# A fourth buffer for r, k, v and the turned r, and flag sums placed among the last products

## The chip, the core and the metric

The kernel runs on one core of a Trainium2 chip. The metric is the device time of one execution in microseconds. TensorE is called PE here, VectorE DVE, ScalarE ACT, GpSimd POOL and SyncE SP. Each runs its own instructions in the order in which they were written and waits for the others through semaphores. SP issues nearly all of the DMAs, in one queue; POOL issues the scatters.

## What is computed

Three layers in a row: a linear attention with a decaying state (one state matrix for each batch and head), a softmax-weighted layer with a norm, and a mixture of eight experts of which each token takes one.

```python
for t in range(S):                       # B, H, S, D = 4, 8, 768, 48
    cur = np.einsum('bhd,bhe->bhde', u[None] * kt, vt)
    y[:, :, t] = np.einsum('bhd,bhde->bhe', rt, state + cur)
    state = w[None, :, :, None] * state + np.einsum('bhd,bhe->bhde', kt, vt)
...
h = x @ w_in                             # x: 3072 x 384, h: 3072 x 1024
solu = h * softmax(h)
x = ((solu - mean) / sqrt(var + 1e-6) * g_ln) @ w_out
...
e = argmax(x @ w_gate)                   # 8 experts
out = gate * (relu(x @ w1[e]) @ w2[e])
```

## The kernel before

The 3072 tokens are cut into 24 tiles of 128. For each tile i the rows of r, k and v come in one DMA (`load_rkv`, line 173, 576 KB) into one of three tiles `rkv0` to `rkv2`, and r, turned so that the head's elements lie on the partitions, comes in another (`load_r`, line 177, 256 KB) into one of three tiles `rT0` to `rT2`. Tile i takes buffer i mod 3. The last of the `rT` tiles serves once, at the start, as scratch for the table of decay powers (`tables`, line 368, turned by PE at line 374).

What happens to a tile: k is scaled by powers of the decay (`kp`, line 414, mostly on POOL) and turned on PE (line 454, copied by ACT at line 461 into `kT`); rT is scaled (line 457, mostly POOL); PE makes the scores (line 470), DVE masks them (lines 476 and 478), PE makes the output (`attend`, lines 500 to 507) and the update of the state (line 518), DVE advances the state (lines 526, 528) and writes the output (`av`, lines 428, 512). ACT squares the rows of r, k, v for a check of their size (line 411; DVE takes some of them at line 408). Then y is split into two half-precision parts (`yy`, lines 541 and 545) and turned by a DMA transpose on SP (line 549); `mm1` (line 576, 18 products of 512 columns) and, after the softmax and the norm, a second DMA transpose on SP (line 652) and `mm2` (line 678, 24 products of 392 columns) follow. The row of each token is scattered to its expert (line 729). In the first 90 us w_in and w_out are loaded by SP (line 187), checked, converted and folded by ACT, DVE and PE. The split of w_in into two half-precision parts is line 235 on DVE.

The nine groups of experts come after: 256 rows and the rest of the expert that stands first, then seven further experts, each with first products (line 977), the rectified halves `hh` (ACT, line 988) and `hl` (DVE, line 991, called rlo in the plan), second products (lines 1002 and 1020), a scaling on ACT (line 1008) and a scatter by POOL (line 1052).

At the end a flag says if any check failed. `marks2` (lines 812 to 816, DVE) brings the checks of each partition together, `flags2` (line 820, PE) sums them over the partitions, `judge2` (lines 824 to 831, DVE) makes the flag `fli`. Every engine loads the flag (line 1426) and branches on it (line 1428) past a slower way of computing everything, to the end of the program (line 1595).

What sets the order: before anything is issued, a planner (`plan`) takes all operations with their costs, dependencies and a due time (`first`). Among the operations that could start within a short time of the earliest it takes the one with the smallest due time, and the resulting order is that of the instructions on each engine. Its dependencies for a load are written with the tables' numbers (`X["rkv"]` and `X["rT"]`, both 3): the load of tile i may come after the last readers of tile i-3. The real wait of a load is set later, by the tile that it writes. On SP the loads stand in one queue with the loads of weights and both kinds of transposes.

## Time and profile before

| What | Value |
|---|---|
| Median of 3 runs | 563.65 us (559.81 to 568.21) |
| The profiled execution | 562.63 us |
| Its span, first to last instruction | 560.9 us |
| PE busy, share of the span | 529.7 us, 94% |
| DVE busy | 424.2 us, 76% |
| ACT busy | 396.0 us, 71% |
| POOL busy | 263.2 us, 47% |
| Mean granted clock of TensorE | 0.982 |

The span is what the profile covers; the execution's own time is 1.7 us longer. The busy time of PE is that of products whose ends are modelled. A wait is put down to what ended last before the waiting instruction began. "kp" and "rT" are names of tiles, "mm" is either of the first two layers' products, "emm" an expert's.

### The profile page before, as it was taken

The page shows a single profiled execution, that of the slowest core. Times are in us where ns is not written, and L with a number is a line of the kernel's source. Part 1 is how long each engine was busy: PE and PEld are TensorE (multiplying, and loading weights), DVE is VectorE, ACT ScalarE, POOL GpSimd, SP SyncE. Part 2 cuts the span into 40 slices and gives each one's busy share as a digit, 9 for nine tenths or more (in the row PEclk, how much of TensorE's full clock was granted, in tenths as well). Part 3 has the DMA queues.
Part 4 walks back from the last instruction along what each step waited for, and adds up shares of the span by engine and source line. Part 5 has one row for each costly group of instructions (what it writes and reads, how often), then busy time and mean ns, then how long its engine had stood idle before and what let it go on. Part 6 is the DMA issues. An engine that isn't in the chain of part 4 may idle for free.

```text
span 560.9 us, 10536 instructions
## 1 busy us (share of the span) xinstructions
PE 529.7 (94%) x3867; PEld 350.1 (62%) x3867; DVE 424.2 (76%) x718; ACT 396.0 (71%) x780; POOL 263.2 (47%) x265
## 2 busy tenths in 40 slices
PE   4899999999999999989999999999999999999990
PEld 2787675655767666666665567864555555666770
DVE  7789899998888979999976866566696787744120
ACT  4968987988677685766765874998696978596220
POOL 5346765977988867768952230130013303050310
PEclk9899989999999999999999999999999999999996
DMA  8576793577765685648459726875698986791100
GB/s 284 200 194 205 249 224 98 117 158 143 203 143 142 130 181 128 159 116 151 98 91 185 201 87 205 262 196 179 164 238 195 251 220 168 198 281 48 36 16 25
DMA packets 116396, 92.17 MB, mean 164 GB/s; under 512 B 92284, under 2 KB 102486, under 8 KB 115952
## 3 DMA queue, kind: packets, MB, share of 16 engines
q1 hardware_dynamic: 111376, 81.93, 57.9%
q0 software_dynamic: 4960, 9.49, 5.5%
q8 instruction: 32, 0.52, 0.4%
q14 instruction: 28, 0.23, 0.1%
HBM read 57.19 MB, written 12.55 MB: 124 GB/s over the span
## 4 chain that ended last, share of the span: by engine, by line
PE 68%; DVE 13%; ACT 6%; DMA 5%; issue 5%; POOL 1%; SPq 0%; ACTq 0%; DVEq 0%; POOLq 0%
PE emm L977 16%; PE mm L678 12%; PE mm L576 11%; PE emm L1020 8%; PE emm L1002 7%; PE scores L470 3%; PE attend L504 2%; PE attend L507 2%; PE update L518 2%; DMA rkv<-in_rkv 2%; DVE yy L545 1%; DMA stage<-in_moe_w 1%; DMA xg<-xs 1%; DMA raw<-in_moe_w_out 1%; DVE vl L449 1%
## 5 line engine op out<-in xcount | busy, mean ns | idle before, releaser
L1052 POOL DMA_INDIRECT out<-o,gt x29 | 37.7, 1299 | 171.6 <-ACT o L1048 97.4
L678 PE MATMUL mm<-wo,zT 128*128 128x392 f16 x576 | 99.3, 329 | 0.5 <-ACT kT L461 0.5
L977 PE MATMUL emm<-exT,w1h 128*128 128x256 f16 (+8 forms) x432 | 98.6, 317 | 0.3 <-DVE hl L991 0.3
L576 PE MATMUL mm<-wi,xT 128*128 128x512 f16 x432 | 97.6, 380 | 0.6 <-DVE AT L478 0.6
L678 PEld LDWEIGHTS <-zT 128*128 128x128 f16 x576 | 54.9, 98 | 38.6 <-issue 1.5
L576 PEld LDWEIGHTS <-xT 128*128 128x128 f16 x432 | 41.8, 99 | 48.1 <-issue 2.0
L977 PE MATMUL emm<-exT,w1l 128*128 128x256 f16 (+8 forms) x216 | 68.5, 317 | 0.0
L977 PEld LDWEIGHTS <-w1h 128*128 128x128 f16 x432 | 41.7, 97 | 25.3 <-issue 0.5
L991 DVE SCALAR_TENSOR_TENSOR hl<-emm,hh 128x928 f16<-128x928 f32 (+8 forms) x32 | 32.2, 1006 | 30.6 <-ACT hh L988 30.6
L988 ACT ACTIVATE hh<-emm 128x928 f16<-128x928 f32 (+8 forms) x32 | 27.1, 847 | 22.0 <-PE emm L977 21.7
L486 POOL TENSOR_TENSOR al<-AT,ah 128x1024 f16<-128x1024 f32 x16 | 37.0, 2311 | 7.1 <-ACT ah L482 6.9
L869 DVE SCALAR_TENSOR_TENSOR w2l<-stage,w2h 128x768 f16<-128x768 f32 x32 | 30.1, 952 | 11.5 <-ACT w2h L865 11.5
L457 POOL TENSOR_TENSOR rT<-rT,trT 128x512 f32<-128x512 f32 x21 | 28.6, 1362 | 21.0 <-DMA rT<-in_rT 16.5
L729 POOL DMA_INDIRECT xs<-row,pos x24 | 28.4, 1185 | 20.7 <-ACT pos L725 12.7
L869 DVE SCALAR_TENSOR_TENSOR w1l<-stage,w1h 128x1024 f16<-128x1024 f32 x24 | 29.3, 1222 | 10.2 <-ACT w1h L865 10.0
L504 PE MATMUL attend<-sdec,rT 128*128 128x96 f32 x160 | 34.1, 298 | 0.0
L1002 PE MATMUL emm<-w2h,hl 128*128 128x384 f16 (+3 forms) x104 | 33.9, 326 | 0.0
L414 POOL TENSOR_TENSOR kp<-rkv,tkm 128x384 f32<-128x384 f32 x23 | 25.1, 1093 | 18.7 <-DMA rkv<-in_rkv 14.8
L1002 PE MATMUL emm<-w2l,hh 128*128 128x384 f16 (+3 forms) x104 | 33.9, 326 | 0.0
L1002 PE MATMUL emm<-w2h,hh 128*128 128x384 f16 (+3 forms) x104 | 33.9, 326 | 0.0
L648 DVE SCALAR_TENSOR_TENSOR z<-e,z 128x1024 f16<-128x1024 f32 x22 | 33.2, 1509 | 0.3 <-ACT z L609 0.3
L470 PE MATMUL scores<-rT,kT 64*128 64x128 f32 x384 | 29.4, 296 | 4.2 <-ACT kT L461 3.4
(260 smaller groups left out, 1357.0 us busy)
## 6 DMA issues: line engine op xcount, KB each, us to landing
rkv<-in_rkv SPq DMA_DIRECT2D x24, 576.0 KB, 4.4
stage<-in_moe_w SPq DMA_DIRECT2D x16, 768.0 KB, 5.6
stage<-in_moe_w SPq DMA_DIRECT2D x8, 1024.0 KB, 5.2
rT<-in_rT SPq DMA_DIRECT2D x24, 256.0 KB, 4.0
stage<-in_moe_w SPq DMA_DIRECT2D x8, 512.0 KB, 4.7
raw<-in_moe_w_in SPq DMA_DIRECT2D x3, 1024.0 KB, 9.0
raw<-in_moe_w_out SPq DMA_DIRECT2D x4, 768.0 KB, 6.0
xs<-zf SPq DMA_DIRECT2D x8, 337.8 KB, 5.6
```

Source lines behind the costliest of these rows:

```text
L470: T.matmul(ps[:, a, j * P:(j + 1) * P], kT[h, j, :], rT[h, j, :], start=True, stop=True)
L486: on[0].tensor_tensor(al, tk.pop(("at", i)), tk["ah", i], op=ALU.subtract)
L504: T.matmul(ps[:, j * 96:j * 96 + 96], rT[:, j, :], sdec[:, j].rearrange("p a d -> p (a d)"), start=True, stop=False, skip_group_check=True)
L576: T.matmul(ps[:, n, :], x[a][:, j, :], wi[b][:, j, n * 512:(n + 1) * 512], start=(j == 0 and m == 0), stop=(j == KD - 1 and m == 2))
L648: V.scalar_tensor_tensor(z[:, 1, :], tk.pop(("e", i)), tk["st", i][:, 10:11] if i is None else ZC, z[:, 0, :], op0=ALU.mult, op1=ALU.subtract)
L678: T.matmul(ps[:, 0:OW], zz[:, a, c, :], wo[b][:, c, :], start=(c == 0 and m == 0), stop=(c == KF - 1 and m == 2))
L869: V.scalar_tensor_tensor(lo, d[:, x], (S1, S2)[m - 1], hi, op0=ALU.mult, op1=ALU.subtract)
L977: T.matmul(ps[:, x, :].rearrange("p (j t) -> p j t", t=d["n"]), a[:, j, fc * P:(fc + 1) * P], d["xT"][:, 0:d["nt"], b, j, 0:d["n"]], start ...
L991: V.scalar_tensor_tensor(cols(d, "hl", q), d.pop(("pm", q)), 0.0, cols(d, "hh", q), op0=ALU.max, op1=ALU.subtract)
L1002: T.matmul(ps[0:n, 0:DM], a[:, c, j * n:j * n + n], b[:, c, :], start=(c == 0 and m == 0), stop=(c == KF - 1 and m == 2))
L1020: T.matmul(ps[:, 0:d["nr"]], a[:, c, m * P:(m + 1) * P], b[:, c, :], start=(c == 0 and x == 0), stop=(c == KF - 1 and x == 2))
L1052: G.indirect_dma_start(out=apart["out"].pop(0), out_offset=bass.IndirectOffsetOnAxis(ap=d["gt"][0:n, j, 1:2].bitcast(U32), axis=0), in_=d. ...
```

## The change

It gives the rows of r, k, v and the turned r one more buffer each, while the planner's dependencies keep the number three. The tables' scratch is the last of the `rT` tiles, so now the fourth. The marks get a dependency on the last rlo of the last expert and a smaller planned cost; the flag sums and the judgement get a due time of -1e9, which puts them ahead of all that could start at the same time.

```diff
-    whole = [one.tile([P, 3, H, D], F32, name=f"rkv{i}") for i in range(X["rkv"])]
-    turned_r = [one.tile([P, 4, P], F32, name=f"rT{i}") for i in range(X["rT"])]
+    whole = [one.tile([P, 3, H, D], F32, name=f"rkv{i}") for i in range(X["rkv"] + 1)]
+    turned_r = [one.tile([P, 4, P], F32, name=f"rT{i}") for i in range(X["rT"] + 1)]
...
-        t = rkv[i] = whole[i % X["rkv"]]
+        t = rkv[i] = whole[i % len(whole)]
...
-        tk["rT", i] = turned_r[i % X["rT"]]
+        tk["rT", i] = turned_r[i % len(turned_r)]
...
-    op("marks2", "dve", 3.5, [... ["marks", "judge"] ...], marks2, first=0)
-    op("flags2", "pe", .3, ["marks2"], flags2, bank="s", until=["judge2"], first=0)
-    op("judge2", "dve", 1.0, ["flags2"], judge2, first=0)
+    op("marks2", "dve", 1.7, [... ["marks", "judge", ("rlo", E, 3)] ...], marks2, first=0)
+    op("flags2", "pe", .3, ["marks2"], flags2, bank="s", until=["judge2"], first=-1e9)
+    op("judge2", "dve", 1.2, ["flags2"], judge2, first=-1e9)
```

On SP the order of the instructions is the same in both kernels; what differs is the buffer that a load writes and what it waits for. SP's queue near the program's start, before (`DMAHW` semaphores tell of landed DMAs, the others of the engine's instructions):

```order
L173 DMA rkv2_144<-in_rkv 128x1152
L187 DMA raw_256<-in_moe_w_in 128x2048 [waits DMAHW0_49]
L177 DMA rT2_147<-in_rT 128x512 [waits DMAHW1_49,DVE_49,PE_49]
L187 DMA raw_329<-in_moe_w_in 128x2048 [waits DMAHW2_49,DMAHW3_49,DVE_49,Activation_49]
L173 DMA rkv0_142<-in_rkv 128x1152 [waits DVE_49,Pool_49]
L177 DMA rT0_145<-in_rT 128x512 [waits DMAHW4_49]
L177 DMA rT1_146<-in_rT 128x512 [waits DMAHW5_49,DMAHW6_49,PE_49,Pool_49]
L187 DMA raw_433<-in_moe_w_out 128x2x768 [waits DMAHW0_49,DVE_49,Activation_49]
L173 DMA rkv1_143<-in_rkv 128x1152 [waits DMAHW7_49,DVE_49]
```

The same rows of the changed kernel:

```order
L173 DMA rkv2_144<-in_rkv 128x1152
L187 DMA raw_258<-in_moe_w_in 128x2048 [waits DMAHW0_49]
L177 DMA rT2_148<-in_rT 128x512 [waits DMAHW1_49]
L187 DMA raw_331<-in_moe_w_in 128x2048 [waits DMAHW2_49,DMAHW3_49,DVE_49,Activation_49]
L173 DMA rkv3_145<-in_rkv 128x1152
L177 DMA rT3_149<-in_rT 128x512 [waits DMAHW4_49,PE_49]
L177 DMA rT0_146<-in_rT 128x512 [waits DMAHW5_49,PE_49,Pool_49]
L187 DMA raw_435<-in_moe_w_out 128x2x768 [waits DMAHW0_49,DMAHW6_49,DVE_49,Activation_49]
L173 DMA rkv0_142<-in_rkv 128x1152 [waits DMAHW7_49,PE_49,Pool_49]
```

The third rT no longer waits for the tables' scratch on DVE and PE, the fourth load of rows waits for nothing, and from there on each load writes the buffer of the tile four back.

On PE one row moves. Before, at the end of the last expert's second products (`hl` and `hh` are the halves of the hidden layer, `fli` the flag):

```order
L1002 LDWEIGHTS hl
L1002 MATMUL emm_6368<-w2h,hl 114x384
L820 MATMUL flags_6398<-g_100,mask 128x47
L1426 TENSOR_LOAD fli
L1428 COMPARE_AND_BRANCH
```

In the changed kernel, after the first 24 of these 72 products:

```order
L1002 LDWEIGHTS hl
L1002 MATMUL emm_6293<-w2h,hl 114x384
L820 MATMUL flags_6340<-g_100,mask 128x47
L1002 LDWEIGHTS hh
L1002 MATMUL emm_6344<-w2h,hh 114x384
```

The sums now stand ahead of 48 products; the load of the flag follows PE's last product. On DVE, ACT and POOL the order is the same as before.

## Rows read from the trace of the kernel before

**Rows 1.** The page: the span

```profile
span 560.9 us, 10536 instructions
```

**Rows 2.** Busy us by stretch: length, PE, PEld, DVE, ACT, POOL; PEclk, DMA, GB/s

```profile
20.00:340.00 320.00, 313.46 (x2531) 213.27 (x2531) 283.41 (x481) 236.37 (x529) 211.14 (x203) 0.98 0.64 153
...
79.00:87.00 8.00, 8.00 (x38) 5.46 (x39) 7.97 (x12) 5.98 (x10) 6.94 (x5) 0.57 0.70 174
40.00:60.00 20.00, 19.66 (x162) 15.74 (x161) 19.66 (x27) 16.33 (x37) 13.63 (x11) 1.00 0.66 206
```

**Rows 3.** PE's waits, 15 to 340 us: who for whom, us, times, longest

```profile
PE scores L470 <- ACT kT L461: 3.4, 3, 1.6
...
PE ktrans L454 <- POOL kp L414: 0.3, 1, 0.3
...
PE rank L712 <- DVE oh L698: 0.2, 1, 0.2
```

**Rows 4.** Waits in SP's queue, the whole span; same columns

```profile
SPq L173 <- DVE av L428: 11.7, 3, 7.8
...
SPq L177 <- PE rank L713: 0.4, 1, 0.4
```

**Rows 5.** POOL's timeline: start, us, instruction, idle time before it and its releaser

```profile
26.49 1.01 POOL L414 TENSOR_TENSOR kp<-rkv,tkm 128x384 f32<-128x384 f32 x1 [7.83 <-DMA rkv<-in_rkv]
...
43.93 1.00 POOL L414 TENSOR_TENSOR kp<-rkv,tkm 128x384 f32<-128x384 f32 x1 [1.93 <-DMA rkv<-in_rkv]
```

**Rows 6.** The chain that ended last, near 176 us: start, us, what

```profile
175.23 1.22 SPq L549
...
176.54 4.71 DMA rkv<-in_rkv
```

**Rows 7.** Timelines of SP's queue and of PE near 40 us

```profile
37.01 1.03 SPq L177 DMA_DIRECT2D rT<-in_rT  x1
39.08 0.33 SPq L173 DMA_DIRECT2D rkv<-in_rkv  x1
...
44.98 0.66 PE L454 MATMUL ktrans<-ident,kp 128*128 128x128 f32 x4 [0.34 <-POOL kp L414]
```

**Rows 8.** Timelines of DVE, PE, POOL and the chain, at the program's end

```profile
535.85 11.71 PE emm L1002 x72
...
539.03 0.14 DVE L816 TENSOR_REDUCE g<-low 128x1 f32<-128x2 f32 x1
...
547.38 0.32 PE L820 MATMUL flags<-g,mask 128*128 128x47 f32 x2
...
548.80 0.15 DVE L831 CAST fli<-fl 128x1 int32<-128x1 f32 x1
...
548.51 1.13 POOL L1052 DMA_INDIRECT out<-o,gt  x1 [2.76 <-ACT o L1008]
```

**Rows 9.** Lines 1426, 1428, 1595 and the scatters: count, ns min/median/max, starts

```profile
L1426 POOLq TENSOR_LOAD <-fli x1: 508/508/508, 549.0 to 549.0; - x1
...
L1428 POOLq EVENT_SEMAPHORE  x6: 17/30/43, 553.9 to 554.3; - x6
...
L1428 POOLq INC_SWDGE_SEM  x1: 1244/1244/1244, 554.4 to 554.4; - x1
...
L1595 POOLq DRAIN  x3: 44/107/4402, 555.7 to 560.7; - x3
...
DMA to landing us min/median/max: 3.7/3.7/5.4
```

**Rows 10.** Timelines of POOL and DVE: the split of w_in

```profile
17.38 1.28 POOL L457 TENSOR_TENSOR rT<-rT,trT 128x512 f32<-128x512 f32 x1 [0.94 <-DMA rT<-in_rT]
...
18.11 1.63 DVE L235 SCALAR_TENSOR_TENSOR wi<-tmp,wi 128x1024 f16<-128x1024 f32 x1
...
42.34 1.21 DVE L235 SCALAR_TENSOR_TENSOR wi<-tmp,wi 128x1024 f16<-128x1024 f32 x1
```

**Rows 11.** The chain: the folding of w_out

```profile
77.41 2.77 PE wout_fold L275 x24
```

More of the change, by code (lines that the diff above doesn't have):

```diff
@@ L1284, in body @@
                 esends.append(("esend", y, j))
-    op("marks2", "dve", 3.5, [k for k in ops if stem(k) == "look"] + [("square", i) for i in range(NT)] + [("hvar", i) for i in range(NT)] + ["marks", "judge"] + [("rhi", y, q) for y in range(E + 1) for q in range(4)] + [("wsq", e, n) for e in range(E) for n in range(4)] + [("xsq", y) for y in range(E + 1)] + [(q, x) for x in range(2) for q in ("woq", "wiq")], marks2, first=0)
-    op("flags2", "pe", .3, ["marks2"], flags2, bank="s", until=["judge2"], first=0)
-    op("judge2", "dve", 1.0, ["flags2"], judge2, first=0)
+    op("marks2", "dve", 1.7, [k for k in ops if stem(k) == "look"] + [("square", i) for i in range(NT)] + [("hvar", i) for i in range(NT)] + ["marks", "judge", ("rlo", E, 3)] + [("rhi", y, q) for y in range(E + 1) for q in range(4)] + [("wsq", e, n) for e in range(E) for n in range(4)] + [("xsq", y) for y in range(E + 1)] + [(q, x) for x in range(2) for q in ("woq", "wiq")], marks2, first=0)
+    op("flags2", "pe", .3, ["marks2"], flags2, bank="s", until=["judge2"], first=-1e9)
+    op("judge2", "dve", 1.2, ["flags2"], judge2, first=-1e9)
     PORT = {"rev", "elo", "wlo", "ylo", "vlo", "zlo", "bits", "wil", "wol", "alo", "decay", "kpow", "ruk", "aval"}
```

## The prediction

> **What bounds the kernel now.** I read the page first, then the busy time of each engine by stretches, the waits of PE and of SP's queue, the chain that ended last, and timelines where a load is late. The span is 560.9 us [rows 1]; the profiled execution took 562.6 us, so 1.7 us lie around the span, and the median of the three runs, 563.65, is 1.0 above that execution. Between 20 and 340 us, where the tiles of r, k, v are used, PE is busy for 313.46 of 320 us [rows 2]. That is the figure to hold on to: nothing that loads data earlier can give PE back more than 320 - 313.46 = 6.5 us in this stretch. The list of what PE waited for there [rows 3] names no DMA at all: eleven entries, 8.6 us together, from 3.4 (the scores, for k turned on ACT) to 0.2 (the one-hot row from DVE). The one that stands behind a load is kp from POOL, 0.3 us.
>
> The loads do wait, and long. SP's queue stands 11.7 us before loads of rkv (line 173) for a reader on DVE [rows 4]; the thirteen entries of lines 173 and 177, down to 0.4, come to 53.4 us, in an order that SP keeps. So the question is who needs what stands behind them. POOL does: it idles 7.83 us before the fourth tile's kp [rows 5]. But POOL has room (13.63 of 20 us even between 40 and 60 [rows 2]), and PE's list has no wait for that kp: PE is still at the products of the tiles ahead when it comes. The chain of waits spends 4.71 us in one piece on rkv [rows 6], which looks like the prize. It is not: that load was issued at 176.54, right after a transpose of yy that SP began at 175.23 and that took 1.22 us; it waited for its place in the queue, not for a buffer. A fourth buffer doesn't move it, since SP's order is the same.
>
> **The fourth buffer, part by part.** It adds no instruction and removes none; each load's wait moves from the readers of tile i-3 to those of tile i-4, and the order is still planned with three. The rows of order show it: the fourth load now waits for nothing new, the fifth rT for a product of tile 0 instead of tile 1.
>
> Going along the loads that stood for a buffer, I find one place where PE profits. The sixth tile was issued at 39.08 after a wait; POOL could begin its kp at 43.93 [rows 5], and PE idled 0.34 us before turning it, at 44.98 [rows 7]. Without the wait the load follows SP's entry of 37.01, which ends at 38.04 (37.01 + 1.03), so it starts 1.0 us earlier. Kp comes 1.0 us earlier, which is more than 0.34, and PE gains 0.34 us. ACT's squares come earlier too, at no gain, since DVE is what is full there: 19.66 of 20 us between 40 and 60 [rows 2]. What follows on PE starts 0.34 us earlier, the first product with w_in among it, whose end releases a transpose on SP and, behind it, a load of w_out; so the shift is carried on and not lost. All other earlier loads I cost at nothing: their cover is POOL's own idle time, and PE's and DVE's work in order. If that cover were gone, what could come is bounded by the 6.5 us above. I take 0.34 because the nearest row is one of PE itself.
>
> **The flag sums.** Two matrix instructions, 0.32 us together at 547.38 [rows 8], move from behind the last product to the place between the first and the second 24 of the 72 last products. Before, the chain was: sums, eight small DVE instructions, the flag written at 548.95 (548.80 + 0.15), all five engines load it at 549.0 and branch [rows 9]. Now two checks are due. First, are the marks ready? Their last DVE instruction ends at 539.17 (539.03 + 0.14). The 72 products fill 11.71 us from 535.85, so 24 of them take 3.90 and end at 539.75. The sums have some 0.5 us in hand, less a semaphore's way; PE should not stand. DVE's order is the same in both kernels, so the marks' new link to the last rlo moves nothing, and behind the marks DVE has only the flag to make. Second, the sums now stand in front of 48 products: the last product, the scaling on ACT and the last scatter come later by what the sums occupy. The bounds are 0 (hidden under the weight loads) and 0.32; I take 0.2, since two full-precision weight loads do not fit quite under one another.
>
> The gain: the flag is known near 541.4 (539.75 + 0.3 + 1.3, the 1.3 as from 547.6 to 548.95), so SP and DVE load and branch some 7 us earlier. PE, ACT and POOL cannot: their own last work stands ahead of the load in their queues. POOL starts the last scatter at 548.51 and loaded the flag at 549.0 while that scatter still ran, so it is held by the scatter's start alone; with the 0.2 it starts at 548.7 and can branch 0.3 us earlier. Behind the branch POOL's next entry comes at 553.9, 4.3 us after it. Then a 1.24 us queue step and a 4.40 us drain close the program [rows 9]. The last scatter's landing, 5.4 us after its issue, ends at 553.9 too. So two things end together there, and the branch alone can give only a little. Bounds: a loss of 0.3 (landing later by the inserted sums, nothing else faster); and a gain of 1.8, if the landing takes the 3.7 us of the other two scatters (548.7 + 3.7 = 552.4, against 553.9: 1.5), POOL's branch keeps up with it, and the 0.3 of the branch comes on top. I take 0.5, nearer to the low end: POOL's 0.3 is worked out from its own rows and the faster landing is only possible, and the drain behind both is untouched.
>
> **Sum.** 562.6 - 0.34 - 0.5 = 561.8 for an execution like the profiled one, and 1.0 more, 562.8, beside a median like that of before. I say **562.0 us**. Against a measurement that can tell about 2% from no change (11.3 us here), that is no difference.
>
> **Where a rule speaks against it.** The moved POOL work is the risk. DVE's split of w_in took 1.63 us at 18.11 while POOL multiplied rT (17.38 to 18.66), and the same split 1.21 us at 42.34, where POOL stood idle until 43.93 [rows 5, 10]: 0.42 us for one overlap. From 26 to 54 us some ten POOL instructions of tiles 3 to 6 can come earlier, under a DVE that is full. They overlap DVE work where they stand today as well, so only the difference counts; if all ten were new overlaps, DVE would lose 4.2 us. The Trainium skill, SBUF — State Buffer, section "Who interferes with whom", says that a DVE instruction with two SBUF inputs and a GpSimd instruction that reads SBUF exclude each other for the whole instruction. By that rule each overlap could cost a whole POOL instruction, about 1.0 us as a kp takes [rows 5], and the sum would be 561.8 + 10 = 571.8; by the row it is 561.8 + 4.2 = 566.0 at most, and the row decides.
>
> **The rivals.**
> 1. *The earlier loads free much more.* If the idle time of PE between 20 and 340 us were all late data in disguise, 6.5 us go: 562.6 - 6.5 - 0.5 = 555.6; half of it gives 558.8. For it: 53.4 us of waits in SP's queue, and 7.83 us of POOL's idle time. Against it: PE's waits name ACT, DVE and POOL results that come late because DVE is full, not because data are. Chance 0.15.
> 2. *Nothing moves.* The order planned with three keeps loads behind transposes, the closing ends with the drain either way: 562.6, within 0.3. For it: 0.09 us before the load at 176.54. Chance 0.25.
> 3. *Slower: POOL's earlier work meets a full DVE.* Place: 15 to 60 us; price 0.42 us an overlap; it decides from the third new overlap on, as then 1.26 us exceed the 0.84 of gains. With eight, 561.8 + 3.4 = 565.2. For it: DVE at 19.66 of 20. Against it: today's places overlap already. Chance 0.12.
> 4. *PE's clock falls elsewhere.* From 79 to 87 us the granted clock is 0.57 [rows 2], its lower level 1.2 GHz for most of it, from the time on that PE had spent 2.77 us on 24 narrow products that fold w_out, from 77.41 [rows 11]; at 2.4 GHz throughout it would have cost (1 - 0.57) x 8 = 3.4 us less. The changed timing can lose or repeat such a stretch: 558.4 or 565.2. Chance 0.08, both signs.
>
> My forecast, the small gain (561 to 562.5), has 0.40; the rivals have 0.60. **Range 557.5 to 566.5**: it takes in rival 1 up to some two thirds, rivals 2, 3 and 4, and the 1.0 us between the execution and the median. The likeliest case alone is 560.5 (562.6 - 0.34 - 1.8) to 563.6 (562.6 - 0.34 + 0.3 + 1.0). Faster by over 2% (below 552.4) needs more than all of PE's idle time there together with the best closing, 6.5 + 1.8 = 8.3 us: 0.04. Slower by over 2% (above 574.9) needs rival 3 at the rule's price for every overlap and more: 0.03. Within 2%: 0.93.
>
> **What would show it.** Right: POOL's 7.83 us before kp go; PE loses its 0.34 us at 45 us; PE between 20 and 340 us stays busy for 313 to 314 us; the sums stand near 539.7 with no idle time on PE ahead of them; the flag is loaded by SP and DVE near 541.5; the drain of 4.4 us is still there. Wrong: the chain's piece on rkv vanishes, or PE's count of waits falls by several us (rival 1); DVE's splits between 15 and 60 us grow from 1.21 to 1.6 us and the stretch ends later (rival 3); PE stands ahead of the sums; or the drain shrinks with the earlier branch, which I hold for fixed.

## The result: 0.9% slower

The changed kernel takes 568.24 us (median of 18 runs, from 565.21; the kernel before beside it 563.62, also 18). The ratio is 1.0086, with a 95% interval of 1.0061 to 1.0112: 4.8 us lost, where I had forecast 562.0 us and a range that ends at 566.5. The ratios in this document leave out executions that were over 1.5% above the fastest of their kernel (four of the twelve of rT_only, three of the thirteen of before_nokeep, elsewhere at most two); medians are over all. The profiled execution took 568.89 us, its span is 567.1, its mean granted clock 0.975 (0.982 before).

What the fourth buffers were to do, they did. The waits in SP's queue, after (columns as in [rows 4]; the list names no others of lines 173 and 177):

```profile
SPq L173 <- POOL kp L414: 0.7, 2, 0.4
SPq L173 <- PE keep L1303: 0.2, 1, 0.2
```

Before, the thirteen waits of these lines came to 53.4 us [rows 4]; now it is 0.9. The busy time by stretch, after (as [rows 2]):

```profile
20.00:340.00 320.00, 313.96 (x2495) 213.38 (x2495) 285.50 (x463) 236.31 (x528) 213.91 (x202) 0.97 0.63 152
40.00:60.00 20.00, 20.00 (x133) 16.27 (x132) 18.05 (x22) 14.15 (x32) 11.56 (x10) 0.74 0.51 173
79.00:87.00 8.00, 8.00 (x60) 6.42 (x58) 7.49 (x13) 7.14 (x15) 5.32 (x6) 0.87 0.99 186
```

PE is as busy as before (313.96 us against 313.46 [rows 2]), and yet gets less done: between 40 and 60 us its records hold 133 matrix instructions where they held 162, because the granted clock is 0.74 where it was 1.00. The products with w_in of the first tile, eighteen of them, start later and run longer. PE's timeline, before and then after:

```profile
39.85 0.98 PE L500 MATMUL attend<-uw,pr 128*128 128x2 f32 x8
...
45.48 4.05 PE L576 MATMUL mm<-wi,xT 128*128 128x512 f16 x18
```

```profile
39.19 1.05 PE L500 MATMUL attend<-uw,pr 128*128 128x2 f32 x8 [0.94 <-DVE pr L424]
...
47.83 5.55 PE L576 MATMUL mm<-wi,xT 128*128 128x512 f16 x18
```

They start 2.35 us later and take 1.5 us longer. Ahead of them stands a wait that the kernel before did not have: PE idles 0.94 us before the fourth tile's attend, for pr from DVE. Even so attend starts 0.66 us earlier than before (39.19 against 39.85): up to there PE is ahead. From 40.6 to 50.9 us the clock is then at its lower level, 1.2 GHz. From attend to the products with w_in it takes 8.64 us in place of 5.63, with no wait on PE in between, so in these two executions the products come late by the lower clock alone. By the fourth tile's first product with w_in the kernel is 5.3 us behind (78.0 against 72.7 us); it keeps some 3.6 us of that up to the experts (first expert product 339.0 against 335.4; behind the fourth tile's first product the kernel before still has 6.83 us at the lower clock, from 79.7 us on [rows 2], and the changed one 3.41, from 85.0).

Why is pr late, when its loads are early? DVE's timeline, before and then after, the instructions that turn the weights' words (L207 to L235), with the reduction L408 and the product L424 that makes pr:

```profile
34.78 0.68 DVE L207 TENSOR_SCALAR tmp<-raw 128x1024 int32<-128x1024 int32 x1
35.50 1.23 DVE L209 SCALAR_TENSOR_TENSOR tmp<-raw,tmp 128x1024 int32<-128x1024 int32 x1
36.64 1.35 DVE L408 TENSOR_REDUCE chm<-rkv 128x1 f32<-128x1152 f32 x1
37.90 0.68 DVE L424 TENSOR_TENSOR pr<-ktrans,rT 128x512 f32<-128x512 f32 x1
...
39.56 1.22 DVE L211 SCALAR_TENSOR_TENSOR tmp<-raw,tmp 128x1024 int32<-128x1024 int32 x1
```

```profile
34.32 1.02 DVE L207 TENSOR_SCALAR tmp<-raw 128x1024 int32<-128x1024 int32 x1
35.37 1.90 DVE L209 SCALAR_TENSOR_TENSOR tmp<-raw,tmp 128x1024 int32<-128x1024 int32 x1
37.20 1.34 DVE L408 TENSOR_REDUCE chm<-rkv 128x1 f32<-128x1152 f32 x1
38.46 0.68 DVE L424 TENSOR_TENSOR pr<-ktrans,rT 128x512 f32<-128x512 f32 x1
...
40.11 2.03 DVE L211 SCALAR_TENSOR_TENSOR tmp<-raw,tmp 128x1024 int32<-128x1024 int32 x1
...
43.46 1.84 DVE L235 SCALAR_TENSOR_TENSOR wi<-tmp,wi 128x1024 f16<-128x1024 f32 x1
```

Four instructions that took 0.68 + 1.23 + 1.22 + 1.21 = 4.34 us (the last of them in [rows 10]) take 1.02 + 1.90 + 2.03 + 1.84 = 6.79. The first two alone make pr 1.0 us later than it could be, and that is about PE's new 0.94 us. (Beside the kernel before, pr starts only 0.56 us later, 38.46 against 37.90, and PE was ready for attend 1.6 us sooner, at 38.25.) POOL's timeline says what lies beside them, after:

```profile
24.59 1.87 POOL L414 TENSOR_TENSOR kp<-rkv,tkm 128x384 f32<-128x384 f32 x1 [5.86 <-PE update L518]
...
33.48 1.31 POOL L418 TENSOR_TENSOR ru<-rkv,ub 128x384 f32<-128x384 f32 x1
34.87 1.33 POOL L420 TENSOR_TENSOR ru<-ru,rkv 128x384 f32<-128x384 f32 x1
39.79 1.27 POOL L457 TENSOR_TENSOR rT<-rT,trT 128x512 f32<-128x512 f32 x1 [3.60 <-DMA rT<-in_rT]
41.51 1.50 POOL L414 TENSOR_TENSOR kp<-rkv,tkm 128x384 f32<-128x384 f32 x1 [0.44 <-DMA rkv<-in_rkv]
43.15 1.07 POOL L441 TENSOR_TENSOR av<-rkv,au 128x384 f32<-128x384 f32 x1
```

and before:

```profile
36.45 1.13 POOL L414 TENSOR_TENSOR kp<-rkv,tkm 128x384 f32<-128x384 f32 x1 [3.03 <-DMA rkv<-in_rkv]
37.54 1.00 POOL L418 TENSOR_TENSOR ru<-rkv,ub 128x384 f32<-128x384 f32 x1
38.62 1.01 POOL L420 TENSOR_TENSOR ru<-ru,rkv 128x384 f32<-128x384 f32 x1
```

The fifth tile's load, now early, lets POOL make ru from 33.48 to 36.20, right beside L207 and L209. With three buffers the same two instructions ran from 37.54 on, beside L408, L424 and others that took no longer for it. POOL's idle time was not spare: it was the time in which these DVE instructions ran at their own length. The same happens twice more (the sixth tile's rT beside L211, av beside L235).

At the program's end, line 820 (the sums), the last scatter and the flag, after (as [rows 8] and [rows 9]):

```profile
L820 PE MATMUL flags<-g,mask x2: 205/240/276, 546.9 to 547.0; 128*128 128x47 f32 x2
...
L1052 POOL DMA_INDIRECT out<-o,gt x29: 952/1072/2104, 355.7 to 556.0; - x29
...
L1426 POOLq TENSOR_LOAD <-fli x1: 495/495/495, 555.7 to 555.7; - x1
...
L1595 POOLq DRAIN  x3: 44/107/4402, 561.9 to 566.8; - x3
```

The sums stand where they were put, with no idle time on PE ahead of them. From the last scatter's start to the span's end it is 567.1 - 556.0 = 11.1 us, against 560.9 - 548.51 = 12.4 before [rows 8].

### The profile page after: what moved, and what is told of

It reads as the page before. It is cut to its first block, busy times and chain, and to the rows that moved or that the text cites. A ratio compares the mean times of both kernels' runs of the same rounds, so it can differ in the third digit from the quotient of the medians.

```text
span 567.1 us, 10518 instructions
## 1 busy us (share of the span) xinstructions
PE 535.0 (94%) x3867; PEld 354.0 (62%) x3867; DVE 429.2 (76%) x718; ACT 396.3 (70%) x780; POOL 265.0 (47%) x265
## 4 chain that ended last, share of the span: by engine, by line
PE 56%; DVE 16%; issue 12%; ACT 6%; DMA 6%; POOL 3%; SPq 0%; POOLq 0%; DVEq 0%; ACTq 0%
PE mm L678 13%; PE mm L576 12%; PE emm L977 9%; PE emm L1020 7%; DMA stage<-in_moe_w 3%; PE scores L470 3%; POOL out L1052 2%; PE attend L504 2%; PE attend L507 2%; PE update L518 2%; DVE yy L545 2%; DMA oh<-oturn 1%; PE ktrans L454 1%; PE emm L1002 1%; DVE AT L478 1%
## 5 line engine op out<-in xcount | busy, mean ns | idle before, releaser
L1052 POOL DMA_INDIRECT out<-o,gt x29 | 36.2, 1247 | 177.0 <-ACT o L1048 100.7
L576 PE MATMUL mm<-wi,xT 128*128 128x512 f16 x432 | 100.4, 388 | 1.2 <-DVE AT L478 1.1
L576 PEld LDWEIGHTS <-xT 128*128 128x128 f16 x432 | 42.5, 100 | 50.3 <-issue 5.6
L414 POOL TENSOR_TENSOR kp<-rkv,tkm 128x384 f32<-128x384 f32 x23 | 26.7, 1163 | 18.2 <-PE update L518 13.1
L582 DVE TENSOR_REDUCE st<-mm 128x1 f32<-128x1024 f32 x24 | 29.2, 1218 | 7.5 <-PE mm L576 5.5
```

The lines of the kernel that those rows point to most:

```text
L576: T.matmul(ps[:, n, :], x[a][:, j, :], wi[b][:, j, n * 512:(n + 1) * 512], start=(j == 0 and m == 0), stop=(j == KD - 1 and m == 2))
L582: V.tensor_reduce(st[:, 0:1], tk["h", i], op=ALU.max, axis=AX.X, negate=True)
L1052: G.indirect_dma_start(out=apart["out"].pop(0), out_offset=bass.IndirectOffsetOnAxis(ap=d["gt"][0:n, j, 1:2].bitcast(U32), axis=0), in_=d. ...
```

## The experiments

Three theories came first. **A**: the earlier loads let PE run ahead of DVE, it idles before the fourth tile's attend, and the granted clock falls. **B**: the flag sums cost it. **C**: it is where the buffers lie in memory. Each part of the change alone, then.

**buffers_only**, the fourth buffers without the flag sums:

```
-    whole = [one.tile([P, 3, H, D], F32, name=f"rkv{i}") for i in range(X["rkv"])]
-    turned_r = [one.tile([P, 4, P], F32, name=f"rT{i}") for i in range(X["rT"])]
+    whole = [one.tile([P, 3, H, D], F32, name=f"rkv{i}") for i in range(X["rkv"] + 1)]
+    turned_r = [one.tile([P, 4, P], F32, name=f"rT{i}") for i in range(X["rT"] + 1)]
...
-        t = rkv[i] = whole[i % X["rkv"]]
+        t = rkv[i] = whole[i % len(whole)]
...
-        tk["rT", i] = turned_r[i % X["rT"]]
+        tk["rT", i] = turned_r[i % len(turned_r)]
```

> The fourth buffers alone, with the flag sums where they were before. In the profiled execution of the change the granted clock is at its lower level for 10.2 us from 40.6 us on, where before had none, and the same DVE instructions stand 3.5 us later after it than before it. Theory A (the earlier loads let PE run ahead of DVE, PE idles before the product of the fourth tile and the clock falls): slower than before by 3.5 to 6 us, ratio 1.006 to 1.011, with a stretch at the lower clock between 38 and 52 us. Theory B (the flag sums are what costs): 562 to 564, ratio 0.997 to 1.001. Theory C (the larger pool puts the experts' tiles in other places and they wait for other readers): slower by 3 to 5 us, all of it after 400 us.

568.95 us, ratio 1.0119 (1.0078 to 1.0160). The whole loss is there, with the same wait of PE (0.81 us at 39.14) and the same stretch at the lower clock (40.1 to 50.3 us).

**flags_only**, the three changed lines of the planner's operations (marks2, flags2, judge2) on three buffers:

```
-    op("flags2", "pe", .3, ["marks2"], flags2, bank="s", until=["judge2"], first=0)
+    op("flags2", "pe", .3, ["marks2"], flags2, bank="s", until=["judge2"], first=-1e9)
```

> The flag sums alone, with three buffers. In the changed kernel's trace the part behind the last products is about 1.1 us shorter than before. Theories A and C: faster than before by 0.5 to 1.5 us, ratio 0.997 to 0.999, early stretches as before. Theory B: slower by 3 to 5 us, ratio 1.005 to 1.009.

561.58 us, ratio 1.0002 (0.9975 to 1.0029). The line of its last scatters:

```profile
L1052 POOL DMA_INDIRECT out<-o,gt x29: 952/1122/2162, 350.7 to 547.3; - x29
```

Its span is 558.2 us, so the way from the last scatter to the end is 10.9 us, 1.5 shorter than before. That is about what the comparison can tell: its interval is worth 1.4 us downwards and 1.6 upwards. Theory B, which asked for 3 to 5 us more, is out.

**pad_only**, four buffers in memory, the fourth used by no tile (the one borrowed for the tables at the start is turned_r[2], as before):

```
-tT = turned_r[-1]
+tT = turned_r[2]
```

> The fourth buffers are allocated but no tile uses them: the memory is laid out as in the change, the loads wait as before, the flag sums stand as before. Theory A: as before, ratio 0.998 to 1.002. Theory C: slower by 3 to 5 us, ratio 1.005 to 1.009, with PE idling for the experts' rectified halves between 430 and 520 us as in the change (3.6 us there, 0.3 us before).

562.10 us, ratio 0.9984 (0.9958 to 1.0011). Theory C, which asked for 1.005 at least, is out.

**late4**, three buffers for the first eight tiles, four in turn from the ninth on:

```
+        t = rkv[i] = whole[i % 3 if i < 8 else (3, 2, 0, 1)[i % 4]]
...
+        tk["rT", i] = turned_r[i % 3 if i < 8 else (3, 2, 0, 1)[i % 4]]
```

> Three buffers for the first eight tiles, all four from the ninth on (the flag sums as before). Theory A: the early stretch is as before, no stretch at the lower clock between 38 and 52 us, ratio 0.997 to 1.002. Were the loss spread over all tiles (earlier POOL work meeting a full DVE everywhere), the ratio would stay at 1.004 to 1.009.

562.89 us, ratio 0.9997 (0.9964 to 1.0030). From the ninth tile on, earlier loads neither cost nor give anything that the comparison can tell. **early4** is the counterpart, four for the first eight tiles and three after them:

```
+        t = rkv[i] = whole[i % 4 if i < 8 else (i - 8) % 3]
...
+        tk["rT", i] = turned_r[i % 4 if i < 8 else (i - 8) % 3]
```

> Four buffers for the first eight tiles, three go round from the ninth on: the counterpart of late4. Theories A, L and R all put the loss into the first eight tiles: 566 to 570 us, mean clock 0.976 to 0.981, four DVE instructions (L207, L209, L211, L235 of 34 to 45 us) at 6 us or more. If the loss needs the fourth buffer of the later tiles too: under 565 us.

568.38 us, ratio 1.0085 (1.0059 to 1.0111): the loss of the changed kernel (1.0086), all of it made in the first eight tiles.

So theory A was left of the three. But the stretched rows of DVE, seen above, made a rival, theory **R**: rival 3 of the prediction, POOL's moved work under a full DVE. If PE's idle time and the clock behind it were the cause, filling that time would bring the loss back. A wider form of A, theory **L** in the expectations, came with the second of these runs: earlier loads leave PE ahead of DVE and ACT in many places, and the lower clock moves from one to the next.

**buffers_keep**, buffers_only with five thrown-away products ahead of the fourth tile's attend:

```
         rT = tk.pop(("rT", i))
+        if i == 3:
+            for _ in range(5):
+                T.matmul(ps[:, 0:DM], ones16, ones16.unsqueeze(1).to_broadcast([P, 3, P]), start=True, stop=True, skip_group_check=True)
```

> The fourth buffers alone, with five filler products (128x384, thrown away) put on PE ahead of the fourth tile's attend, where buffers_only had PE idle for 0.81 us at 39.14. Two theories of the 7 us that buffers_only costs. Theory A (clock): the idle makes the granted clock fall from 40.1 to 50.3 us, and that is the cost; then the stretch at the lower clock is gone here, the first group of mm products starts at 45 to 46 us and the kernel takes 561 to 564 us, ratio 0.997 to 1.003. Theory R (rival 3 of the prediction): the fourth load, issued earlier, puts POOL's ru work of the fifth tile (33.5 to 36.2 us) beside DVE's first two tmp instructions; the four instructions L207, L209, L211 and L235 of 34 to 45 us take 1.02 + 1.90 + 2.11 + 1.84 = 6.87 us in place of 0.68 + 1.23 + 1.22 + 1.21 = 4.34, on a DVE without idle time; then these 2.5 us stay with the clock at 1.00, products start at 47 or later, and the kernel takes 565 to 567 us.

570.30 us, ratio 1.0168 (1.0123 to 1.0214). The products came too late, behind the wait for pr (0.68 us of idle time stayed), since they write attend's bank: the first of them waited for DVE's pr, as attend does. The experiment is flawed as a filler, and its time lies above what either theory foresaw. The stretch at 40 us is gone from its trace, but one of 10.24 us stands at 64.7 in its place, and the loss remains. **buffers_fill** mends it, with sixteen narrow products behind the fourth tile's update, in a part of its bank that nobody reads:

```
     def update(i, slot):
...
+        if i == 3:
+            for _ in range(16):
+                T.matmul(ps[:, DM:512], ones16, ones16, start=True, stop=True, skip_group_check=True)
```

> buffers_only with sixteen filler products (128x128 f16, thrown away) behind the fourth tile's update, in that update's own bank, so that they wait for nothing and lie in the idle time before its attend (in buffers_keep the fillers stood behind the wait for pr: 0.68 us of idle stayed, a stretch of 10.24 us at the lower clock came at 64.7 instead of 40.1, and the kernel took 570.3 us). Over the runs so far, what the lower clock takes, (1 - mean granted clock) x time, is 8.8 us before, 12.4 in buffers_only and in the changed kernel, 12.1 in rkv_only, 10.2 in rT_only; the rest of the time is 554.0, 556.7, 555.9, 554.4, 555.3. Theory A (the idle at 39 us is the cause of the extra lower clock): mean clock 0.983 to 0.988, 563 to 566 us, where the rest above 562.5 is theory R's (DVE rows stretched beside POOL). Theory L (with earlier loads the order leaves PE ahead of DVE and ACT at many places, and the lower clock moves to the next of them): mean clock 0.976 to 0.981, 567 to 571 us.

573.51 us, ratio 1.0162 (1.0104 to 1.0220). The busy time of each engine from 40 to 51 us (columns as in [rows 2]), of the changed kernel and then of buffers_fill:

```profile
40.00:51.00 11.00, 11.00 (x55) 8.63 (x55) 11.00 (x12) 8.66 (x21) 9.00 (x7) 0.53 0.47 172
```

```profile
40.00:51.00 11.00, 11.00 (x94) 8.50 (x93) 11.00 (x13) 9.34 (x22) 9.39 (x8) 1.00 0.54 171
```

The clock stays up, PE starts 94 matrix instructions in place of 55, and the first products with w_in begin at 44.3 us, earlier than in the kernel before. DVE is full in both, and twelve or thirteen instructions are all that it gets done. PE then stands for late results 20 us later. PE's longest waits from 15 to 95 us in buffers_fill, and the one row in early4, where the clock held at 40 us too:

```profile
PE wout_part L265 <- ACT sto L256: 2.3, 1, 2.3
PE mm L579 <- DVE AT L478: 1.3, 1, 1.3
```

```profile
64.81 1.54 PE L265 MATMUL wout_part<-ident,sto 128*128 128x128 f32 x6 [3.02 <-ACT sto L256]
```

Sto is what ACT makes of w_out's words when DVE has turned them. The lower clock comes there too: 6.83 us from 68.3 on in buffers_fill, 13.65 us from 64.0 on in early4. So theory A falls in its narrow form: the idle time at 39 us and the stretch at 40 us behind it can go, and the loss stays, as waits and lower clock some 20 us later. The mean clock of buffers_fill over its runs, 0.978, is what theory L foresaw (0.976 to 0.981) and not what A did (0.983 to 0.988); its time lies above both. By the ratios buffers_fill is 2.4 us worse than buffers_only, which their intervals do not tell apart.

**rkv_only** and **rT_only**, one kind of buffer each:

> A fourth buffer for the rows of r, k, v alone; the turned r keeps three. Theories A and R both put the loss on the rows' earlier loads: as buffers_only, 566 to 570 us, with a stretch of over 6 us at the lower clock between 38 and 52 us and the four DVE instructions at 6 us or more. If the turned r's loads are what matters, 561 to 564 us.

> A fourth buffer for the turned r alone; the rows of r, k, v keep three. Theories A and R: as the kernel before, 561 to 564 us, POOL's kp and ru of the fifth tile at 36 us or later, no lower clock between 38 and 52 us. If the turned r's loads are what matters (rev on POOL beside DVE), 566 to 570 us.

rkv_only 566.56 us, ratio 1.0074 (1.0039 to 1.0109); rT_only 565.01, ratio 1.0014 (0.9971 to 1.0058). The two intervals overlap, and rT_only's median over all its executions is 0.45% above that of the kernel before beside it (562.47), so rT_only may lose a little too. And **only3**, where of the first eight tiles only the fourth gets the new buffer:

```
+        t = rkv[i] = whole[([0, 1, 2, 3, 1, 2, 3, 1][i] if i < 8 else (0, 2, 3, 1)[i % 4])]
```

> Four buffers, but handed out so that of the first eight tiles only the fourth gets the new one (order 0, 1, 2, 3, 1, 2, 3, 1): its load is issued as early as in the changed kernel, while the loads of the fifth to eighth tile wait for the same tiles as with three buffers; from the ninth tile on four go round. Theory A (PE is early, idles before the fourth tile's attend, and the clock falls): PE still reaches that place about 1.6 us early, the clock falls as in buffers_only, 566 to 569 us. Theory R (POOL's ru of the fifth tile meets DVE): ru waits for its load until 36 us or later as before, the four DVE instructions sum to 4.3 to 4.6 us, pr comes by 38.6 us, no idle of over 0.4 us before attend, no lower clock there, 561 to 564 us.

566.75 us, ratio 1.0070 (1.0035 to 1.0105). Both theories missed here. In only3 the rows are those that R foresaw (0.68 + 1.23 + 1.22 + 1.21 = 4.34 us, no lower clock from 38 to 52 us), and the time is the one that A foresaw; in its profile 10.24 us at the lower clock stand at 17.5 us, ahead of all these rows. In rkv_only neither what A foresaw nor what R foresaw is in the trace: DVE's instructions L207 to L235 of 33 to 42 us last as long as in the kernel before,

```profile
33.09 0.68 DVE L207 TENSOR_SCALAR tmp<-raw 128x1024 int32<-128x1024 int32 x1
33.80 1.23 DVE L209 SCALAR_TENSOR_TENSOR tmp<-raw,tmp 128x1024 int32<-128x1024 int32 x1
```

and the clock is whole from 20 to 60 us, but 6.83 us at the lower level follow from 64.2 us on. Its mean granted clock over twelve runs is 0.979, about as low as that of the changed kernel (0.978). I come back to it below.

At the fourth tile's attend rkv_only is a control that I had not planned:

```profile
38.16 0.98 PE L500 MATMUL attend<-uw,pr 128*128 128x2 f32 x8
```

PE comes there as early as after the change (38.16 against 38.25), finds pr ready and keeps its clock; rT_only shows the same at 38.24. So PE's being early is not enough for the wait of 0.94 us and the stretch behind it: pr has to be late as well, and with DVE's instructions at their own length it is not.

**before_nokeep** was to lower the clock without moving a load: the kernel before without the six filler products around its fourth tile's ktrans and update.

```
     def keep(n, kind, slot):
+        calls.append(n)
+        if len(calls) in (5, 6):
+            return
```

> The kernel before without the six filler products around its fourth tile's ktrans and update (37.19 and 38.13 us); loads and buffers as before. This takes 1.3 us of throw-away work from PE where DVE's pr comes no sooner, so PE idles there by about as much as in the changed kernel. Theories A and L (idle on PE ahead of a full DVE costs through the granted clock): more lower clock, mean clock 0.976 to 0.981, 565 to 569 us, though no load moved. If idle there costs nothing by itself: 561 to 563.5 us at a mean clock of 0.984.

566.59 us, ratio 1.0029 (0.9989 to 1.0069): not decided. Its profile, of the slowest of its executions (575.95 us), has no idle time before that attend (38.97 us); PE stands 1.52 us for POOL's kp at 45.28 instead, so the idle time did not come where it was meant to.

**planned4** lets the planner know of the fourth buffers:

```
-ybuf=10, tmp=1, rkv=3, rT=3,
+ybuf=10, tmp=1, rkv=4, rT=4,
```

> The two numbers rkv and rT in the table set to 4, so that the planner knows of the fourth buffers: it orders loads, fillers and the choices between POOL and DVE for them; no other number is changed. Theory P (the loss is that the order, its fillers too, was made for loads that come late): 558 to 564 us, mean clock at 0.984 or more. If a full DVE is what the earlier loads run into, whatever the order: 565 to 570 us. The other numbers of the table were chosen with three, so that a loss here alone doesn't refute theory P.

589.42 us, ratio 1.0469 (1.0407 to 1.0530). The order differs in hundreds of rows on every engine, and the sixth tile's products with w_in start at 131.5 us (90.6 before). The planner's other numbers belong to its order with three; the run says that much, and nothing on theory P.

The last two runs were to put theory R to the test in both directions. **buffers_hold** keeps the early loads and holds four POOL instructions back by data, each by a copy of one column of what DVE writes:

```
     def kpow(i):
+        if i == 4:
+            G.tensor_copy(held[:, 0:1], raw["f", 2][0][:, 0:1])
+        if i == 5:
+            G.tensor_copy(held[:, 1:2], wi[1][:, 2, 0:1])
...
     def rev(i):
+        if i == 4:
+            G.tensor_copy(held[:, 2:3], wi[1][:, 1, 0:1])
+        if i == 5:
+            G.tensor_copy(held[:, 3:4], raw["f", 2][0][:, 0:1])
```

> buffers_only with its loads as early as there, but with four POOL instructions held back by data: rev of the fifth and sixth tile and kp of the fifth and sixth wait, through a copy of one column, for the DVE instruction on the weights (L235, L211, L209, L235) that they ran beside in buffers_only and stood clear of with three buffers. The first 84 instructions of DVE are the same ones in every kernel of this study but planned4, and take 44.0 us in the kernel before and 48.7 in buffers_only, since those beside POOL are stretched. Theory R (the loss begins with DVE stretched by POOL work that the late loads had kept apart from it): the 84 take 44 to 45.5 us, L209 and L211 of 34 to 42 us 1.25 us each, and the kernel takes 561 to 565 us. Theory L (PE ahead of DVE and ACT, whatever their speed, and the clock): DVE as said, but 566 to 570 us at a mean clock of 0.976 to 0.981.

564.57 us, ratio 1.0041 (1.0007 to 1.0075). POOL's, DVE's and PE's timelines (the new lines shift the numbers: L420 is kp, L510 the attend):

```profile
36.70 0.18 POOL L417 COPY held<-tmp 128x1 f32<-128x1 f32 x1 [5.66 <-DVE tmp L209]
36.84 1.00 POOL L420 TENSOR_TENSOR kp<-rkv,tkm 128x384 f32<-128x384 f32 x1
```

```profile
34.69 0.68 DVE L207 TENSOR_SCALAR tmp<-raw 128x1024 int32<-128x1024 int32 x1
35.41 1.23 DVE L209 SCALAR_TENSOR_TENSOR tmp<-raw,tmp 128x1024 int32<-128x1024 int32 x1
```

```profile
40.12 0.98 PE L510 MATMUL attend<-uw,pr 128*128 128x2 f32 x8
```

POOL stands 5.66 us there until L209 has ended, and the kernel is faster than buffers_only for it: about two thirds of what that one lost is back (1.0119 to 1.0041, and the intervals just do not meet), and the mean granted clock over the runs is 0.983 again, where buffers_only had 0.978 and the kernel before 0.984. DVE's first 84 instructions take 45.6 us, a little over the 44 to 45.5 foreseen, as L211 took 1.50 us beside ru. So POOL's early work is what costs most of the loss. By which way it does, the run does not show alone: kp, held back, holds PE back too, whose attend starts at 40.12 (39.85 before), so PE's being ahead is gone together with DVE's stretching.

**before_pool** leaves all loads late and gives POOL six products of 1.0 us, thrown away, in its idle time:

```
     def rev(i):
         on[0].tensor_tensor(tk["rT", i], tk["rT", i], trT, op=ALU.mult)
+        for _ in range({3: 1, 4: 3, 5: 2}.get(i, 0)):
+            G.tensor_tensor(idle, tkm, tkm, op=ALU.mult)
```

> The other direction: the kernel before, loads and buffers untouched, with six POOL products of 128x384 (thrown away, 1.0 us each) put into POOL's idle time: one behind rev of the fourth tile, three behind that of the fifth (33.4 to 36.4 us, where DVE runs L207 and L209), two behind that of the sixth (42 to 44 us, beside L235). Theory R: the first 84 instructions of DVE take 45.5 to 48 us in place of 44.0, and the kernel takes 564.5 to 568 us. If DVE's stretching is hidden and only the loads' timing matters: 561 to 564 us.

568.26 us, ratio 1.0093 (1.0053 to 1.0133), just above what R foresaw: a loss like that of the changed kernel, from POOL work alone and without any earlier load. DVE's first 84 instructions take 47.5 us, as foreseen. Its timelines of POOL and of DVE:

```profile
36.48 3.02 POOL L461 TENSOR_TENSOR idle<-tkm 128x384 f32<-128x384 f32 x3
39.46 1.44 POOL L414 TENSOR_TENSOR kp<-rkv,tkm 128x384 f32<-128x384 f32 x1
40.86 1.98 POOL L418 TENSOR_TENSOR ru<-rkv,ub 128x384 f32<-128x384 f32 x1
```

```profile
39.20 0.84 DVE L207 TENSOR_SCALAR tmp<-raw 128x1024 int32<-128x1024 int32 x1
40.08 1.90 DVE L209 SCALAR_TENSOR_TENSOR tmp<-raw,tmp 128x1024 int32<-128x1024 int32 x1
```

The three products pushed kp and ru onto L207 and L209, which take 0.84 and 1.90 us as after the change. Part of its delay is a later kp, for which PE waited 2.59 us at 51.35, so the 1.0093 is not all DVE's. And this profile, of 571.57 us, says little of the clock: 10.24 us at the lower level begin at 17.8, while the first added product starts at 31.71. Up to there the instructions are those of the kernel before, whose profile has 3.41 us, from 21.6. So much can differ between two executions of the same instructions, and the table below gives the clock as a mean over the runs.

All kernels with DVE's instructions in the same order, beside one another. The DVE sum is that of the durations of its first 114 instructions (to about 72 us) in the one profiled execution; the first 84 (to about 48 us) are those of the expectations; the clock is the mean over the runs compared.

| Kernel | DVE sum, us | first 84, us | ratio | mean clock |
|---|---|---|---|---|
| late4 | 68.7 | 43.6 | 0.9997 | 0.987 |
| pad_only | 68.9 | 43.8 | 0.9984 | 0.987 |
| before | 69.1 | 44.0 | 1 | 0.985 |
| before_nokeep | 69.6 | 43.5 | 1.0029 | 0.984 |
| flags_only | 70.3 | 44.5 | 1.0002 | 0.985 |
| rkv_only | 71.0 | 43.4 | 1.0074 | 0.979 |
| rT_only | 71.9 | 44.7 | 1.0014 | 0.985 |
| only3 | 72.6 | 45.0 | 1.0070 | 0.983 |
| buffers_hold | 73.1 | 45.6 | 1.0041 | 0.983 |
| before_pool | 73.6 | 47.5 | 1.0093 | 0.981 |
| buffers_only | 73.9 | 48.7 | 1.0119 | 0.978 |
| the changed kernel | 74.9 | 48.3 | 1.0086 | 0.978 |
| buffers_fill | 75.3 | 47.1 | 1.0162 | 0.978 |
| buffers_keep | 75.4 | 47.5 | 1.0168 | 0.979 |
| early4 | 76.4 | 48.2 | 1.0085 | 0.979 |

The kernels with sums up to 70.3 us are within 0.3% of the kernel before; the six from 73.6 on lose 0.85 to 1.7%; those between lie between, though not in strict order. rkv_only does not fit: its first 84 instructions take the least of all, and it loses 0.7%. The lower clock goes along with the loss, rkv_only's too. Over the runs, the changed kernel has 2 x (0.985 - 0.978) x 567 = 8 us more at 1.2 GHz than the kernel before, which takes at most half of that, 4 us, of PE's work. Within the 4.8 us, the lower clock can therefore be the larger part. That it follows from PE running dry at a late DVE is seen at 40 us in two profiles (after, buffers_only); for the other stretches it is argued and not shown.

## Why the prediction was wrong

**The step that failed** is "All other earlier loads I cost at nothing: their cover is POOL's own idle time, and PE's and DVE's work in order." The cover was there, but I had looked only at who waits for the loads, and not at what POOL does when it gets its data: it works beside DVE, and DVE's instructions take longer. What the runs showed in place of nothing: the earlier loads alone cost 1.19% (buffers_only), DVE's four instructions from 34 to 45 us took 6.79 us in place of 4.34, and with POOL held back about two thirds of the loss were gone (buffers_hold). The 7.83 us of idle time before the fourth tile's kp [rows 5], which I took for harmless cover, became 5.86, now for a product of PE; the rT products behind that kp then ran beside DVE's next split, which took 2.30 us at 27.70 where it had taken 1.36:

```profile
26.42 2.50 POOL L457 TENSOR_TENSOR rT<-rT,trT 128x512 f32<-128x512 f32 x2
```

```profile
27.70 2.30 DVE L235 SCALAR_TENSOR_TENSOR wi<-tmp,wi 128x1024 f16<-128x1024 f32 x1
```

**Rival 3 named the right mechanism at the wrong price.** I had the place (15 to 60 us), the victim (DVE, 19.66 of 20 us [rows 2]) and the row of one overlap: 1.63 us at 18.11 against 1.21 [rows 10]; the sign that I had named for it, splits of 1.6 us, came (1.84 at 43.46, 2.30 at 27.70). I took the difference, 0.42 us, as the price of any overlap, and let that row decide against the rule of the Trainium skill. It was not a price but one case. POOL's rT ran from 17.38 to 18.66 [rows 10], so it had 0.55 us left when the split began at 18.11, and 0.55 + 1.21 = 1.76, which is the measured 1.63 but for 0.13. The rows of after follow the same sum:

| DVE instruction, start | POOL has left | alone | sum | measured |
|---|---|---|---|---|
| L207, 34.32 | 33.48 + 1.31 - 34.32 = 0.47 | 0.68 | 1.15 | 1.02 |
| L209, 35.37 | 34.87 + 1.33 - 35.37 = 0.83 | 1.23 | 2.06 | 1.90 |
| L211, 40.11 | 39.79 + 1.27 - 40.11 = 0.95 | 1.22 | 2.17 | 2.03 |
| L235, 43.46 | 43.15 + 1.07 - 43.46 = 0.76 | 1.21 | 1.97 | 1.84 |

Each is the sum less 0.13 to 0.16. In these rows the one that comes second waits until the other has ended, and then takes its full time; POOL does the same (kp at 41.51 has to let L211 end at 42.14: 0.63 + 1.00 = 1.63, measured 1.50). The Trainium skill, SBUF — State Buffer, section "Who interferes with whom", says this: the shared port pair is an exclusive lock, held for the whole instruction, and the other engine blocks. These rows agree with it but for the 0.13 to 0.16 us, and the prediction should not have set one row against it. The same section says that a reduction never contends on this chip, and that two inputs count only if both lie in SBUF. The trace agrees: L408 took 1.35 us beside POOL's kp and 1.34 without, and L424, one of whose inputs comes from PSUM, 0.68 beside POOL's ru and 0.68 without.

The overlaps made the first 84 DVE instructions (to about 48 us) 48.3 - 44.0 = 4.3 us longer and the first 114 by 5.8 us, where I had allowed 4.2 at the very most. "Against it: today's places overlap already" was half right: the sums before hold some overlaps, but from 34 to 43.5 us DVE lost only 0.26 us to them (L545 at 41.62: 0.80 us, 0.54 after the change).

**Rivals 3 and 4 came together.** I gave the clock a rival of its own, of either sign, at 3.4 us and a chance of 0.08. In the changed kernel's profile they come one behind the other: a late DVE makes PE stand 0.94 us, then 10.24 us at the lower level follow. Two rivals that come together add up, and the range (566.5 at the top) held each only singly: 561.8 + 4.2 + 0.5 x 10.24 = 571.1 would have been the sum of both. My sign that PE stays busy for 313 to 314 us came true and told nothing: a product at half the clock counts as busy too.

**The 0.34 us at the sixth tile** did not appear. The wait for kp at 44.98 [rows 7] is gone from PE's list, but only since PE comes there 1.9 us later. Kp itself begins 2.4 us earlier (41.51 against 43.93 [rows 5]), more than the 1.0 that I had, and it helps nobody, since PE, at the lower clock, comes to turn it only at 46.92.

**The bound of 6.5 us on any gain** was not put to the test, as no kernel gained. The reading of the piece of 4.71 us on rkv as no prize [rows 6] held: after the change the same piece takes 4.73 us, again right behind a transpose, and late4, with four buffers from the ninth tile on, is at 0.9997.

**The closing** went as foreseen (SP and DVE loaded the flag at 548.5, 6.5 us before PE's last product ended), and my 0.5 us was too low in the profiles: 12.4 us from the last scatter to the end became 11.1, and 10.9 in flags_only, a gain of 1.3 to 1.5 within the bound of 1.8. The drain kept its 4402 ns. PE did not stand for the marks. In times, flags_only's 1.0002 neither shows the gain nor excludes it.

**What stays open.** rkv_only and only3 lose 0.7% with DVE sums near the middle of the table; rkv_only does so with none of the overlaps that cost the changed kernel from 34 to 45 us, and with a low clock (0.979). So earlier loads can cost without a late DVE there, and by what way is not shown. Its profile has 6.83 us at the lower level from 64.2 us on, where rT_only, with nearly the same rows up to there, has none; what makes the clock fall in the one and not in the other no run here tells apart. buffers_hold, which still loses 0.4%, has 6.83 us from 66.5 on as well; this rest was not taken away. How the 4.8 us divide between DVE's lateness, PE's being ahead and the clock stays open. In the profile of after PE also waited 3.6 us for DVE's hl in the experts (0.3 before); buffers_only, as slow, shows 1.8, so I take that for a difference of executions, which was not tested.

## What to carry to other kernels

An engine's idle time can be what keeps a fuller engine fast: before data are brought earlier, list what the idle engine will start on, and what the full one runs at that moment. Price an overlap on shared ports by what the first instruction has left, not by the difference that one example shows. An order planned around late loads can hold separations that nothing in the program enforces; where loads come early, enforce those that matter by data, or leave the buffer out.

## What the hardware showed

- DVE and POOL took turns, but for 0.13 to 0.16 us: the second of two overlapping instructions took its own time plus the rest of the first one, on either engine (the table above).
- Which instructions take part could be read from the rows: one input or two, integer or float, over SBUF (L207, L209, L211, L235) were stretched; a reduction of 1152 columns (1.34 and 1.35 us) and a product with an input in PSUM (0.68 and 0.68) were not.
- Up to 0.94 us of waiting on PE stood ahead of 10.24 us at 1.2 GHz in two profiles, 40.6 to 50.9 us after the change and 40.1 to 50.3 in buffers_only, and the eighteen products took 5.55 us in place of 4.05; in early4 a wait of 0.86 us at the same place was followed by none at that place.
- The same instructions got different clocks: up to 31 us the kernel before and before_pool are the same program, and their profiles have 3.41 us (from 21.6) and 10.24 us (from 17.8) at the lower level.
- POOL loaded the flag at 555.7, ahead of the start of its last scatter at 556.0; before, it loaded it 0.5 us behind that start [rows 8, 9].
